# Block-sorted attention and a ResMLP layer on one core: first batch from flat slabs on 64-row array tiles, later batches in a hand-set order

## The chip, the cores and the metric

One NeuronCore of a Trainium2 chip (trn2) runs one program. The metric is device time in microseconds (us); most runs were timed several times and the median is given. The profiled execution has a *span*, from its first to its last instruction, which is some 1.8 us shorter than its time. The *chain* is the work that ended last, followed back from the last instruction to what released it at each step. A run over 1.5% above the fastest of the same kernel counts as slow, and ratios leave slow runs out. A ratio here is the mean time of one kernel's fast runs over that of the other's in the same rounds, so it is not quite the ratio of the medians beside it.

Engines: PE is TensorE (matmul), PEld its weight loads, DVE VectorE, ACT ScalarE, POOL GpSimd, SP SyncE; a trailing q means the engine's DMA queue or sequencer. Every line of the compute engines says L65 because one helper records every instruction; lines are told apart by tile names.

## The reference

Four batches, 8 heads, 768 tokens, 64 per head; the layer is 512 wide with a hidden width of 2048.

```python
P = sort_net                              # (4, 8, 8, 8); five rounds of exp and normalising
k_sorted = einsum('bhij,bhjcd->bhicd', P, k_b)      # mix the 8 blocks of 96 tokens
v_sorted = einsum('bhij,bhjcd->bhicd', P, v_b)
attn = softmax(scale * q_b @ k_sorted^T)            # within each block of 96
x = attn @ v_sorted                                 # -> (4, 768, 512)
a1 = alpha1 * x + beta1
u  = x + lam * einsum('ts,bsd->btd', w_tok, a1)     # token mixing, 768 x 768
a2 = alpha2 * u + beta2
out = u + lam * (relu(a2 @ w_ch1) @ w_ch2)          # "h" is the first wide layer, "ch" the second
```

`lam` is folded into the second layer's weights: W2 is scaled once, on the chip, before the first ch.

## The kernel before

All of batch 0's attention, the preparation of w_tok and W2 and batch 1's first loads share the first 80 us. After that, layers of one batch alternate with attention of the next.

```python
load_q(0); load_raw(0, 1); load_raw(0, 0)             # GpSimd issues the first loads; k and v go f32 -> f16 in the DMA
...                                                    # w_tok, lam, alpha, beta
load_raw(1, 1); load_raw(1, 0); load_q(1)              # batch 1's data go ahead of the weights
...
def prep_w2(which):                                    # 16 products, all on GpSimd
    for m in which:
        pool.tensor_tensor(W2p[:, m, :], W2p[:, m, :], lamB[:], ALU.mult)
...
def mix_v(b, alone=False, groups=range(6)):            # V mixed, then to DRAM and back,
    ...                                                # which puts it into rows of 96 tokens
    nc.sync.dma_start(vscr[b, ...], vA[...])
    nc.sync.dma_start(Vs[b % NV][...], vscr[b]...)
...
def moe_turn(b, hf, ps=psb):                           # u turned on TensorE, 12 turns a half
    ...
emit_attention(0, between)                             # TensorE order: batch 0, w_tok turns between
...
prep_w2(range(HT))
moe_h(0, 0)
for b in range(1, B):
    ...
    emit_attention(b); moe_h(b - 1, 0); moe_ch(b - 1, 0); moe_h(b - 1, 1); moe_a(b); moe_ch(b - 1, 1)
```

The softmax here doesn't subtract the row's maximum and nothing guards it: scores larger than these inputs give would overflow.

## Time and profile before

| before | value | how to read it |
|---|---|---|
| time, three runs | 305.71 us (302.97 to 307.75) | device time |
| span of the profiled run | 308.3 us | a slow run by the rule: some 310 us of time, over 2% above 302.97 |
| TensorE busy | 276.1 us, 90% | the rest of the span is waiting |
| first h matmul | 59.2 us | from the chain in the prediction below |
| first ch matmul | 77.4 us | start of its second stretch there |
| one steady batch | 64.2 us | third row of its stretches |

Two rows of the page's DMA list matter as well (what was moved, issuing queue, count, size, us from issue to landing): W2's pieces and the way of V back from DRAM.

```profile
W2p<-in_moe_w_ch_dram POOLq DMA_DIRECT2D x4, 512.0 KB, 19.1
Vs_107<-vscr SPq DMA_DIRECT2D x4, 384.0 KB, 7.2
```

The 19.1 us are mostly queueing behind older loads: at the 207 GB/s that the prediction reads from that stretch, 512 KB would take some 2.5 us (an estimate). The median of V's way back is 7.2 us, while the prediction found one of 20.14 us.

### The profile page before, as it was taken

What the parts mean: (1) busy time and instruction counts of PE and PEld (TensorE: products, weight loads), DVE (VectorE), ACT (ScalarE), POOL (GpSimd) and SP (SyncE); (2) the same over time, 40 slices, a digit from 0 to 9 for tenths busy, and PEclk for the clock granted to TensorE, in tenths of its full rate; (3) what the DMA queues carried; (4) which work ended last, traced back from release to release, by engine and by line L of the source; (5) the groups of instructions that cost most, each with busy time, mean ns of one, the idle gap of its engine ahead of it and who ended that gap; (6) DMA issues with size and microseconds to landing.
All of it is one profiled execution on the core that took longest, in us unless ns stands there. A gap on an engine that the chain in (4) does not pass through costs nothing.

```text
span 308.3 us, 5117 instructions
## 1 busy us (share of the span) xinstructions
PE 276.1 (90%) x1965; PEld 164.0 (53%) x1965; DVE 180.5 (59%) x414; ACT 153.3 (50%) x327; POOL 104.2 (34%) x106
## 2 busy tenths in 40 slices
PE   3858997699959998999999989989999889999994
PEld 2547774365527554456755544566646444554641
DVE  7779578699936939669684089295840571001001
ACT  4894854384314555349713745197407450631710
POOL 8514569999540460240019300510085000000000
PEclk9968979699997999999999999999999999999999
DMA  5999999929993210592302002950021002102012
GB/s 198 211 237 257 204 208 205 201 59 125 157 226 126 86 52 0 138 152 21 102 20 86 0 2 65 147 97 0 2 70 37 0 0 70 34 0 79 26 34 68
DMA packets 33208, 29.31 MB, mean 95 GB/s; under 512 B 20184, under 2 KB 28192, under 8 KB 33184
## 3 DMA queue, kind: packets, MB, share of 16 engines
q0 software_dynamic: 8112, 14.82, 24.9%
q1 hardware_dynamic: 25072, 14.17, 23.0%
q8 instruction: 15, 0.25, 0.3%
q14 instruction: 9, 0.07, 0.1%
HBM read 32.78 MB, written 8.65 MB: 134 GB/s over the span
## 4 chain that ended last, share of the span: by engine, by line
PE 63%; DMA 19%; DVE 7%; ACT 5%; POOL 2%; issue 2%; SPq 0%; DVEq 0%; POOLq 0%; ACTq 0%
PE ch_ps L65 25%; PE h_ps L65 24%; DMA Vs_107<-vscr 7%; DMA b1lB<-in_moe_beta_dram 6%; PE tok_ps L65 5%; DMA qn_127<-in_q_dram 3%; PE x_ps L65 3%; ACT kT L65 3%; PE sc_ps L65 3%; DVE toktmp L65 2%; DMA raw_88<-in_v_dram 2%; DVE u_0_723 L65 2%; PE uT_ps L65 2%; DMA vscr<-vA 2%; PE v_ps L65 1%
## 5 line engine op out<-in xcount | busy, mean ns | idle before, releaser
L65 ACT ACTIVATE hTa<-h_ps 128x384 bf16<-128x384 f32 x96 | 46.7, 496 | 60.6 <-PE h_ps L65 59.8
L65 PE MATMUL ch_ps<-W2p,hTa 128*128 128x512 bf16 x288 | 72.4, 382 | 0.0
L65 PEld LDWEIGHTS <-W1p 128*128 128x128 bf16 x512 | 49.6, 99 | 32.0 <-issue 2.8
L65 PEld LDWEIGHTS <-hTa 128*128 128x128 bf16 x288 | 27.5, 99 | 27.3
L65 ACT ACTIVATE et<-sc_ps 96x384 f16<-96x384 f32 x64 | 27.0, 497 | 19.7 <-PE sc_ps L65 19.5
L65 DVE TENSOR_TENSOR toktmp<-tok_ps,a1lB 128x512 f32<-128x512 f32 x24 | 16.5, 686 | 30.6 <-PE tok_ps L65 30.6
L65 DVE CAST kT<-k_ps 64x256 f16<-64x256 f32 x72 | 30.3, 421 | 2.2 <-PE k_ps L65 1.1
L65 ACT CAST kT<-k_ps 64x256 f16<-64x256 f32 x48 | 17.6, 366 | 17.9 <-PE k_ps L65 17.2
L65 PEld LDWEIGHTS <-w_tokT 128*128 128x128 f16 x198 | 17.4, 101 | 15.7 <-issue 1.5
L65 PE MATMUL ch_ps<-W2p,hTb 128*128 128x512 bf16 x96 | 25.1, 379 | 0.0
L65 PEld LDWEIGHTS <-kT 128*96 128x96 f16 x160 | 17.0, 141 | 9.0 <-issue 2.3
L65 POOL TENSOR_TENSOR W2p<-W2p,lamB 128x512 bf16<-128x512 bf16 x16 | 20.5, 1316 | 0.1
L65 PEld LDWEIGHTS <-et 96*96 96x96 f16 x256 | 15.9, 129 | 8.4 <-issue 4.5
L65 DVE RECIPROCAL recip<-x_ps 96x4 f32<-96x4 f32 x64 | 9.9, 169 | 17.2 <-PE x_ps L65 16.9
L65 ACT ACTIVATE hTb<-h_ps 128x384 bf16<-128x384 f32 x32 | 15.7, 491 | 5.9 <-PE h_ps L65 5.3
L65 PEld LDWEIGHTS <-hTb 128*128 128x128 bf16 x96 | 9.3, 98 | 10.5
L65 PE MATMUL h_ps<-a2T_730,W1p 128*128 128x384 bf16 x64 | 14.4, 362 | 0.3 <-ACT a2T_730 L65 0.2
L65 PE MATMUL h_ps<-a2T_2377,W1p 128*128 128x384 bf16 x64 | 12.4, 326 | 0.0
L65 PE MATMUL h_ps<-a2T_1573,W1p 128*128 128x384 bf16 x64 | 12.4, 326 | 0.0
L65 PE MATMUL x_ps<-Vs_107,et 96*96 96x65 f16 x128 | 8.5, 213 | 3.5 <-DMA Vs_107<-vscr 3.4
L65 PE MATMUL h_ps<-a2T_731,W1p 128*128 128x384 bf16 x64 | 10.7, 326 | 0.0
L65 PE MATMUL h_ps<-a2T_1574,W1p 128*128 128x384 bf16 x64 | 10.6, 326 | 0.0
(272 smaller groups left out, 448.6 us busy)
## 6 DMA issues: line engine op xcount, KB each, us to landing
out_dram<-ost SPq DMA_DIRECT2D x24, 192.0 KB, 2.2
qf<-in_q_dram SPq DMA_DIRECT2D x8, 384.0 KB, 5.1
vscr<-vA SPq DMA_DIRECT2D x6, 384.0 KB, 4.4
W1p<-in_moe_w_ch_dram POOLq DMA_DIRECT2D x4, 512.0 KB, 14.6
W2p<-in_moe_w_ch_dram POOLq DMA_DIRECT2D x4, 512.0 KB, 19.1
Vs_107<-vscr SPq DMA_DIRECT2D x4, 384.0 KB, 7.2
out_dram<-ost SPq DMA_DIRECT2D x24, 64.0 KB, 2.0
wt_109<-in_moe_w_tok_dram POOLq DMA_DIRECT2D x1, 864.0 KB, 15.7
```

Of the source, the lines that this page charges most:

```text
L65: ins = getattr(self.eng, name)(*args, **kwargs)
```

## The change

The intent is an earlier start of the wide layers and fewer TensorE cycles per batch. Batch 0 is loaded as flat slabs and turned, mixed and scored on 64-row tiles of the array, two at once, with *filler* matmuls on zeros (`warm`) wherever TensorE would wait. Batch 1's loads move behind the weights. W2's scaling is split between GpSimd and VectorE. Later batches still mix k and turn q on TensorE; u is now turned in the DMA, the scores run on 64-row tiles, and every small piece is hung by hand behind a chosen piece of a wide layer (`put`). The diff, cut:

```diff
-    load_q(0)
-    load_raw(0, 1)
-    load_raw(0, 0)
+    load_slabs(q8, q)
+    load_slabs(k8, k)
+    load_halves(v8, v[0])
+    for half in range(2):          # w_tok in two halves; the second lives in the buffer of "qn"
+        t_ = att.tile([128, 3, S], F16, name="wt16", tag=("mixed", "qn")[half], bufs=1)
...
+    def warm(n):
+        ps = pse([128, 512], FT, "warm_ps")
+        for _ in range(n):
+            pe.matmul(ps[:], wz[:, 0:128], wz[:], start=True, stop=True)
+
+    def turn_slab(src, rhs, g, name, ps):            # 24 matmuls of 64x64, alternating tiles
+        for s in range(12):
+            for h2 in range(2):
+                t = (s + 6 * h2) % 12
+                r = slice(h2 * 64, h2 * 64 + 64)
+                pe.matmul(ps[r, t // 6, ...], src[r, g, t * D:(t + 1) * D], rhs(r, g), ...)
+
+    def v_sort(n, eng):                              # v: token-major to column-major, a quarter
+        eng(
+            VD[:, n * 16:(n + 1) * 16, 0:HB].rearrange("p d t -> p t d"),
+            v8[:, :, n * 16:(n + 1) * 16],
+        )
...
-    def moe_turn(b, hf, ps=psb):                     # 12 turns on TensorE
+    def moe_cross(b, hf):
+        for m in range(3):
+            nc.sync.dma_start_transpose(uT[:, :, m * 128:(m + 1) * 128], u16_of[b][:, 3 * hf + m, :])
...
+    score(0, 0, 0, psd)
+    k_copy(0, 2, kp2, 1, copy)
+    v_sort(1, act.copy)                              # the four v_sorts alternate with exponentials on ScalarE
+    score(0, 0, 1, psd)
...
+    load_kv(1)
+    load_q(1)                                        # needs the "qn" buffer
...
+    put(0, 0, "h", 6, ... second_u(kt))              # GpSimd: row, then addition, three times
+    put(0, 0, "h", 7, *(lambda n=n: mix_matrix(n) for n in range(1, B)))
+    for n in range(4):
+        put(0, 0, "h", 11 + n, lambda n=n: scale_w2((4 * n, 4 * n + 1), pool),
+                               lambda n=n: scale_w2((4 * n + 2, 4 * n + 3), dve))
+    for b in range(1, B):
+        p = b - 1
+        put(p, 0, "h", 15, lambda b=b: bounce_v(b))  # V to DRAM
+        put(p, 0, "c", 2, lambda b=b: back_v(b))     # and back
+        if b + 1 < B:
+            put(p, 0, "c", 2, lambda b=b: load_kv(b + 1), lambda b=b: load_q(b + 1))
...
```

## The prediction

> **What bounds the kernel now.** I read the page's slices first, then the engines by stretch, then the chain of the start, then GpSimd's timeline.
>
> ```profile
> PE   3858997699959998999999989989999889999994
> PEclk9968979699997999999999999999999999999999
> DMA  5999999929993210592302002950021002102012
> ```
>
> Forty slices of 7.7 us. From the ninth slice (62 us) on TensorE is nearly full but for the twelfth; earlier it has holes and a lowered clock, and the DMA row is full from slice 2 to 8. So there are two regimes, a start bound by something else and a long TensorE-bound rest.
>
> ```profile
> core 0: us, PE busy (x) PEld busy (x) DVE busy (x) ACT busy (x) POOL busy (x), PEclk, DMA share, GB/s
> 30.00:60.00 30.00, 24.05 (x242) 16.85 (x241) 20.96 (x49) 17.95 (x37) 24.08 (x25) 0.87 1.21 208
> 77.40:101.60 24.20, 20.73 (x171) 12.87 (x170) 16.64 (x41) 7.33 (x18) 7.51 (x8) 0.93 0.86 161
> 165.90:230.10 64.20, 62.05 (x438) 35.99 (x436) 38.36 (x87) 33.31 (x73) 16.84 (x13) 1.00 0.29 51
> ```
>
> The last row is one whole batch in the steady state: TensorE idles 2.1 of 64.2 us. There only fewer TensorE cycles can help.
>
> ```profile
> 11.67 18.12 DMA b1lB<-in_moe_beta_dram
> 30.07 10.10 DMA qn_127<-in_q_dram
> 40.45 0.74 POOL W2p L65
> 41.21 1.28 POOL a1lB L65
> 42.49 1.23 POOL b1lB L65
> ...
> 48.44 4.94 DVE u_0_723 L65
> ...
> 59.21 3.04 PE h_ps L65 x9
> ```
>
> The chain of the start (start, us, what). The first wide layer (h) begins only near 59 us, and it is held by GpSimd: its multiplications of two small vectors stand behind weight-DMA issues, which in turn wait for older loads.
>
> ```profile
> 38.59 0.74 POOL L65 DMA_DIRECT2D W2p<-in_moe_w_ch_dram  x1 [1.27 <-DMA qn_127<-in_q_dram]
> 40.45 0.74 POOL L65 DMA_DIRECT2D W2p<-in_moe_w_ch_dram  x1 [1.12 <-DMA qn_127<-in_q_dram]
> 52.92 20.52 POOL L65 TENSOR_TENSOR W2p<-W2p,lamB 128x512 bf16<-128x512 bf16 x16
> ```
>
> GpSimd's timeline. Counting its DMAs in issue order, number n waits for the landing of number n-8 (the W2 issue that is the 28th waits for the 20th, a q half). Then it scales W2 in 16 steps of 1.28 us, until 73.4 us. The second layer (ch), which needs W2, starts at 77.4 us.
>
> **What the Trainium skill says.** "TensorEngine Tiling (Array Packing)", Key Properties: different tiles load weights and multiply in parallel, but changing the tiling mode drains the engine. No 64-row tile runs before, so the trace cannot agree or not. "TensorE: Matmul & The Clock Gate", Part 1: the clock is halved when idle and released by some 3.4 us of activity; the low digits of PEclk in the start agree in kind. "SBUF — State Buffer", Who interferes with whom: a DVE operation with two SBUF inputs contends with GpSimd's reads. The trace agrees: the same 512-wide f32 addition took 4.94 us at 48.4 us, beside GpSimd, and 0.69 us in later batches. "DMA: Bandwidth & Descriptors", Constraints: the transpose in DMA takes 2-byte data and is issued from Sync or Scalar only; no transfer before shows its time.
>
> **The change, part by part.**
>
> *Steady part, TensorE.* A layer half is 64 h matmuls in 10.40 us and 48 ch matmuls in 10.36 us (the chain at 273 to 304 us), so a batch is 4 x 10.4 = 41.5 us; token mixing is 36 x 0.216 = 7.8 us. Neither changes. Before, a batch also has 6 value-mixing matmuls of 512 columns (1.3 us), 24 key-mixing and 24 q-turning ones of 128 columns (about 0.056 us each, 1.35 us each set), 32 scores of 192 columns at 0.08 (2.6), 64 attention-times-V at 0.044 (16 took 0.71 in the chain: 2.8) and 24 turns of u (1.35): 10.7 us. Sum 60.1; the measured 64.2 leaves 4.1 of waits. After, the turns of u go to the DMA for all but the first half of batch 0 (-1.35 us a batch), and the scores become 64 matmuls of half the width on 64-row tiles; at the 0.044 us of the similar V matmuls that is 2.8, the same. So 9.6 us. I add 1.5 us a batch for draining at some 16 changes of tiling mode (an estimate of 0.1 us each: half of the 0.2 us that one short turn takes alone here, as nothing before shows a drain) and 2 us for waits, since h (16 x 0.496 = 7.9 us of ScalarE) now shares its stretch with 8 exponentials of 768 elements (about 0.77 us, by the slope from 384 elements at 0.497 to 512 at 0.588): 14.1 us of ScalarE against 16 us of TensorE is close. A batch becomes about 62.5 us instead of 64.2. The hand-set order mostly fills the same time; it is not a large gain in the steady state, apart from the first V bounce (20.14 us of DMA at 72 to 92 us in the chain), which before left some 3.5 us of hole in TensorE.
>
> *Start, TensorE.* The chain of 5 normalisations of the sort matrix (done at 11.5 us) stays. Flat slabs of batch 0 are turned in 64-row tiles, two at once; v is mixed straight into the V layout (no kT turn, no 4 x 0.69 us copy). I count about 96 q, 96 k, 128 v, 64 score and 96 V small matmuls at 0.035 to 0.044 us (18 us), 54 turns of w_tok at 0.077 (4.2), token mixing with its additions (6), fillers (39 x 0.216 plus a cold first dozen, 10) and 1.5 of the rest: about 40 us from 1.2 us on. So h can start at 40 to 44 us instead of 59. DVE's own sum to there is about 27 us and ScalarE's about 30, so neither is worse. The fillers occupy only time in which TensorE waits; they may cost a little where a release comes early and buy the full clock.
>
> *Start, transfers.* In f32-to-16-bit loads the DMA row runs at about 207 GB/s of destination. q, k, v, w_tok, W1 and W2 are 3 x 0.79 + 1.18 + 2.1 + 2.1 MB, two broadcasts 0.5: 8.3 MB, 40 us, so W2 has landed by about 43 us instead of 60, because batch 1's loads now come after it. Then the halves of batch 1's v land at about 45 and 47, of k at 49 and 51, q at 54.
>
> *Start, GpSimd: where I think the gain is cut.* Batch 1's four k, v and six q issues stand in GpSimd's order ahead of its elementwise work. By the n-8 rule the last q issues wait for the first kv transfers, 47 us. Only then come, for the second half of batch 0, three rows of 1.56 and three additions of 1.16 (8.2 us, to 56) and GpSimd's half of the W2 scaling, 8 x 1.28 = 10.3 us, to about 66.5. The other 8 are DVE's. With h at 42 us, h plus what is hung into it (18 w_tok turns 1.4, column sums 1.04, token mixing 3.9, value mixing 1.3 us) ends at 61; the first ch piece (3.45 us) then waits at its 14th matmul for the scaled W2 until about 67 and ends at 67.6. Before, ch began at 77.4, so its first piece ended at about 81. The start therefore gains 13 us, not the 17 of h.
>
> *Sum.* From 67.6: layers 166 - 10.4 - 3.45 = 152.3; token mixing of three batches 23.6; attention 9.6 x 3 - 1.3 = 27.5; drains 4.5; waits 6. That is 213.9 (before: 223 from the same point). TensorE ends at 281.5; the last addition and store took 4.2 us before. Span about 285.7 against 308.3, ratio 0.927. On the median of 305.71 this is 283; I shade it to 282 because the waits are the softest term.
>
> **Rivals.**
> - *GpSimd does not hold the start.* If its elementwise work comes in time, ch begins when h ends: first piece done at about 64 instead of 67.6, and a faster TensorE start (h at 35 us, tiles truly two at once) then counts fully: 270 to 275. For it: the order was set by hand. Against it: the kernel before has just such a hold on its chain, 18.12 and 10.10 us.
> - *Fillers and mode drains eat the gain.* If each filler delays real work and the small matmuls run at the 0.08 us of those before instead of 0.04, the start needs 55 us and h begins as late as before; with three batches of scores at 0.08 too (+7 us): 295 to 302. Against it: 16 V matmuls took 0.71 us.
> - *The DMA transposes come late.* After the third token piece TensorE has two ch pieces, 6.9 us, until the next h. Multiply 0.69, add 0.70, copy 0.63 and four affine steps of 0.25 leave about 3.9 us for a transfer; out stores took 2.2. If three 128 KB transposes queue for 8 us, each of three batches loses about 4 us: 294.
> - *Scaled W2 or V arrives even later* (batch 1's V bounce meeting batch 2's loads, as in the 20.14 us before): +3 to +8 us.
>
> **Range and chances.** The ideal (no holds, no drains) is near 268; the rivals that add up lie at 294. So 282, with 270 to 293 for eight in ten. To stay within 2% the time would have to exceed 299.6, which needs two of the bad rivals together: 4%; slower by 2%: 1%; faster: 95%.
>
> **What would show it.** The first h matmul at 40 to 44 us; GpSimd idle on batch-1 transfers just ahead of its rows for the second half; its W2 scaling ending at 65 to 68 us and the first ch group waiting on it; ch's first piece done near 68. Steady batches of 62 to 63 us with full clock, no turn of u on TensorE after batch 0, score matmuls at 0.04 us spacing. PEclk near 9 in all early slices. Wrong would be: h later than 48 us, transposes over 4 us with TensorE idle before h, or a steady batch over 64 us.

## The result, and the profile after

| | time, median | fast runs against before | span | TensorE busy |
|---|---|---|---|---|
| before, with the later runs | 306.73 us (302.97 to 313.11) | | 308.3 | 276.1 |
| after, 4 runs | 326.99 us (325.00 to 329.54) | 1.0744, 95% interval 1.0666 to 1.0822 | 323.2 | 279.4 |

The change made the kernel 7% slower. The prediction was 282 us with a range to 293: wrong in its sign.

The slices of the kernel after, 40 of 8.1 us each:

```profile
PE   6964897987089628999999899999998999999994
PEclk9985699799679776999999999999999999999998
DMA  6999992091009991013228990321590013202112
```

From the seventeenth slice on (129 us), TensorE is full. Earlier there are three troughs: slices 3 and 4, with a clock that falls to 5, slices 10 and 11 with an idle DMA, and slices 14 and 15 with a full DMA. The stretches around them (length, then busy us and instructions of PE, PEld, DVE, ACT, POOL, then clock, DMA share, GB/s), with one steady batch last:

```profile
20.00:40.00 20.00, 12.39 (x218) 8.82 (x220) 5.39 (x6) 16.57 (x13) 10.05 (x13) 0.57 1.21 211
...
57.00:90.00 33.00, 20.96 (x145) 11.46 (x146) 23.06 (x37) 9.12 (x20) 26.30 (x22) 0.83 0.43 37
...
102.00:123.00 21.00, 10.43 (x86) 5.78 (x86) 2.14 (x3) 9.35 (x16) 15.60 (x14) 0.77 1.45 177
...
150.30:211.90 61.60, 60.08 (x441) 33.57 (x443) 31.05 (x56) 32.69 (x59) 24.40 (x22) 1.00 0.67 103
```

TensorE idles 7.6, 12.0 and 10.6 us in the first three rows and 1.5 us in the steady batch. A steady batch takes 61.6 us against 64.2 before, with a granted clock of 1.00 in both rows, so the part that was to gain does gain; the loss lies ahead of it. In each trough another engine is busy: ScalarE in the first (16.57 of 20 us), VectorE and GpSimd in the second, the DMA in the third.

**First hold: four copies.** The chain that ended last, from 16.83 us on (start, us, what):

```profile
16.83 3.64 ACT vd L65
20.47 0.64 ACT et L65
21.11 3.53 ACT vd L65
24.64 0.64 ACT et L65
25.28 3.50 ACT vd L65
28.78 0.64 ACT et L65
29.42 3.50 ACT vd L65
32.91 0.65 ACT et L65
```

For 16.7 us the chain never leaves ScalarE. `vd` is the quarter copy of v (`v_sort`), `et` an exponential of the scores. TensorE's v mixing needs `vd`, and its next pieces need a buffer in PSUM, the memory that TensorE writes to, that an exponential has to empty; the trace names `vd` for 5.3 us of weight loads' waiting and `et` for 4.9 us of the v mixing's. The group row gives 3613 ns for one copy:

```profile
L65 ACT COPY vd<-v 128x768 f16<-128x768 f16 x4 | 14.5, 3613 | 0.0
```

The first h matmul comes at 57.25 us instead of the predicted 40 to 44. In the chain:

```profile
57.25 0.81 PE h_ps L65 x4
...
91.56 3.56 PE ch_ps L65 x13
```

The second line ends the first ch piece.

**Second hold: GpSimd's order, and W2 scaled by two engines at once.** GpSimd's timeline (start, us, instruction, and in brackets the idle time before it and what ended it), and below it VectorE's over the same stretch:

```profile
37.80 1.05 POOL L65 DMA_DIRECT2D raw<-in_k_dram  x2
62.76 5.31 POOL L65 DMA_DIRECT2D qn<-in_q_dram  x6 [23.91 <-PE wtok_ps L65]
...
76.07 1.17 POOL L65 TENSOR_TENSOR u<-x,u 128x512 f32<-128x512 f16 x1
77.20 12.11 POOL L65 TENSOR_TENSOR W2p<-W2p,lamB 128x512 bf16<-128x512 bf16 x8
```

```profile
78.83 9.47 DVE L65 TENSOR_TENSOR W2p<-W2p,lamB 128x512 bf16<-128x512 bf16 x6
88.22 1.21 DVE L65 CAST mixed<-mix_ps 128x1024 f16<-128x1024 f32 x1
89.35 1.28 DVE L65 TENSOR_TENSOR W2p<-W2p,lamB 128x512 bf16<-128x512 bf16 x2
```

GpSimd stands for 23.9 us in front of batch 1's q loads, because their destination is the buffer that holds w_tok's second half, and TensorE turns that half only behind the first h pieces (the last turn ends at 62.46). Then follow 5.3 us of issues, three rows and additions, and only at 77.2 us the scaling of W2. It runs beside VectorE's half, at 1545 and 1401 ns per piece. VectorE's copy of the mixed V stands behind its six and TensorE waits for it until 89.5 us; the first ch piece ends at 95.1 us instead of the predicted 67.6.

**Third hold: V's way back.** In the chain it is one piece:

```profile
102.08 20.05 DMA Vs<-vscr
```

The DMA issues between 90 and 130 us (size, median us to landing) show what it shared the engines with:

```profile
raw<-in_v_dram POOLq DMA_DIRECT2D x2, 384.0 KB, 9.2
Vs<-vscr SPq DMA_DIRECT2D x1, 768.0 KB, 20.1
raw<-in_k_dram POOLq DMA_DIRECT2D x2, 384.0 KB, 8.2
qn<-in_q_dram POOLq DMA_DIRECT2D x6, 128.0 KB, 12.1
```

Batch 2's loads, 2.3 MB at their destination, were issued at 96.7 to 110.7 us. TensorE has nothing to multiply the attention with until 122.2.

What held as predicted, or went better: 24 matmuls of 64x64 took 0.49 us on the chain, 0.02 us each where 0.035 to 0.044 was assumed; eight scores with their change of mode take 0.28 to 0.50 us on the chains, mostly 0.31, so 0.04 each; and the DMA transposes land in 2.3 us (at most 4.2), with VectorE waiting for them 13.8 us in all and TensorE never named as waiting for them.

```profile
uT<-u SPq DMA_TRANSPOSE x21, 2.3
```

### The profile page after: what moved, and what is told of

The parts are those of the page before. It is cut to its first block, busy times and chain, and to the rows that moved or that the text cites. A ratio compares the mean times of both kernels' runs of the same rounds, so it can differ in the third digit from the quotient of the medians.

```text
span 323.2 us, 5632 instructions
## 1 busy us (share of the span) xinstructions
PE 279.4 (86%) x2308; PEld 157.5 (49%) x2322; DVE 152.7 (47%) x296; ACT 148.6 (46%) x255; POOL 120.9 (37%) x121
## 4 chain that ended last, share of the span: by engine, by line
PE 71%; ACT 11%; DMA 8%; DVE 5%; POOL 3%; issue 2%; SPq 0%; DVEq 0%; POOLq 0%
PE ch_ps L65 25%; PE h_ps L65 22%; PE tok_ps L65 9%; DMA Vs<-vscr 6%; ACT vd L65 4%; PE x_ps L65 4%; DVE W2p L65 3%; POOL u L65 3%; ACT et L65 2%; PE wtok_ps L65 2%; PE sc_ps L65 2%; DMA q<-in_q_dram 2%; ACT kT L65 1%; PE warm_ps L65 1%; ACT hTa L65 1%
## 5 line engine op out<-in xcount | busy, mean ns | idle before, releaser
L65 PE MATMUL h_ps<-a2T,W1p 128*128 128x384 bf16 x512 | 99.0, 335 | 6.8 <-DVE ost L65 3.2
L65 POOL TENSOR_TENSOR u<-x,u 128x512 f32<-128x512 f16 x24 | 30.8, 1310 | 41.8 <-DVE x L65 38.3
L65 PEld LDWEIGHTS <-hTa 128*128 128x128 bf16 x288 | 28.1, 99 | 32.9 <-issue 2.2
L65 POOL TENSOR_SCALAR u<-b1lB,rs 128x512 f32<-128x512 f32 x21 | 33.0, 1606 | 28.9 <-DVE ost L65 28.9
L65 DVE TENSOR_TENSOR ost<-ch_ps,u 128x512 f32<-128x512 f32 x24 | 16.6, 690 | 48.0 <-PE ch_ps L65 42.9
L65 PE MATMUL tok_ps<-x,w_tokT 128*128 128x512 f16 (+1 forms) x198 | 34.3, 321 | 1.6 <-DVE toktmp L65 1.0
L65 ACT ACTIVATE et<-sc_ps 96x768 f16<-96x768 f32 (+1 forms) x32 | 27.3, 853 | 13.1 <-PE sc_ps L65 12.9
L65 ACT CAST kT<-kmix_ps 64x512 f16<-64x512 f32 x27 | 19.1, 708 | 29.6 <-PE kmix_ps L65 15.2
L65 POOL DMA_DIRECT2D qn<-in_q_dram x18 | 15.9, 913 | 23.9 <-PE wtok_ps L65 23.9
L65 PE MATMUL x_ps<-Vs,et 96*96 96x65 f16 (+2 forms) x288 | 17.8, 210 | 7.4 <-DMA Vs<-vscr 7.4
L65 PEld LDWEIGHTS <-et 96*96 96x96 f16 (+2 forms) x288 | 16.6, 124 | 12.1 <-DMA Vs<-vscr 7.8
L65 DVE TENSOR_TENSOR u<-toktmp,u 128x512 f32<-128x512 f32 x21 | 18.8, 897 | 2.8 <-POOL u L65 0.7
L65 PE MATMUL sc_ps<-qT,kT 64*96 64x96 f16 (+1 forms) x256 | 13.4, 225 | 6.1 <-ACT et L65 4.1
## 6 DMA issues: line engine op xcount, KB each, us to landing
W2p<-in_moe_w_ch_dram POOLq DMA_DIRECT2D x4, 512.0 KB, 16.8
```

The costliest lines, as they stand in the source:

```text
L65: ins = getattr(self.eng, name)(*args, **kwargs)
```

## The experiments

The theory after the result: three holds, (a) the strided v copies on ScalarE, (b) GpSimd's order ahead of W2's scaling, which also lets both halves run at once, (c) the loads beside V's way back, and nothing in the new steady state. The rivals: the fillers or the new array modes cost the time; or the holds hide one another, so that mending one moves the wait to another place. Eleven kernels ran, all correct. In each group "before" was timed on the same chip; its medians there were 310.6, 308.4, 305.4 and 303.9 us, with slow runs among them. The kernel after was not timed again in these groups; a gain in us below is a difference of medians between groups and good to some 1 to 2 us.

### One copy in each form (m1_sorts)

```diff
-        eng(VD[..., quarter n].rearrange("p d t -> p t d"), v8[:, :, quarter n])
+        if n in (0, 2): eng(VD[..., quarter n], v8[:, :, quarter n].rearrange("p t d -> p d t"))
+        else:           eng(VD[..., quarter n].rearrange("p d t -> p t d"), v8[:, :, quarter n])
-    v_sort(2, act.copy)     # and v_sort(3, act.copy)
+    v_sort(2, copy)         # and v_sort(3, copy): VectorE
```

The elements are the same; only the order in which they are visited changes: with contiguous writes the 2-byte reads step by 128 bytes, in the original the writes do.

> A measurement of the disputed cost: the four copies that re-sort the v slab (128x768, 16-bit, SBUF to SBUF) took 3.61 us each on ScalarE in the changed kernel, where I had counted under 0.8. Here the first runs on ScalarE with contiguous writes and strided reads, the second on ScalarE as before (strided writes), the third on VectorE with contiguous writes, the fourth on VectorE with strided writes. Theory 'stride of the write': the first about 0.9 us, the second 3.6, the third 0.9 or less, the fourth over 2 us. Rival 'any stride is slow': all four 3 us or more. Rival 'ScalarE alone is slow': first and second 3.6, third and fourth 0.9. The first h matmul moves from 57 us to 48-52 us if two copies become cheap, and stays at 57 if TensorE itself set the start.

ScalarE's timeline of this run, contiguous writes first, then strided:

```profile
16.97 1.52 ACT L65 COPY vd<-v 128x768 f16<-128x768 f16 x1
...
19.11 3.68 ACT L65 COPY vd<-v 128x768 f16<-128x768 f16 x1
```

And VectorE's, again contiguous first:

```profile
21.48 0.87 DVE L65 COPY vd<-v 128x768 f16<-128x768 f16 x1
...
25.47 1.87 DVE L65 COPY vd<-v 128x768 f16<-128x768 f16 x1
```

On ScalarE strided writes cost 2.4 times as much as strided reads; the contiguous form was expected at 0.9 us and took 1.52. On VectorE one copy each says nothing firm, because contiguous ones took 0.80 to 1.87 us in later runs, and the strided one took 1.87, under the expected 2. The one look took 316.12 us, h began at 48.5 us.

### All four copies on VectorE, contiguous (a_sort)

```diff
-            VD[...].rearrange("p d t -> p t d"), v8[:, :, ...],
+            VD[...], v8[:, :, ...].rearrange("p t d -> p d t"),
-    v_sort(0, act.copy)     # and 1, 2, 3
+    v_sort(0, copy)         # and 1, 2, 3
```

> Only the four v copies change: VectorE instead of ScalarE, with contiguous writes (0.87 us there in the measurement, against 3.61). Theory 'ScalarE's copies set the start': h begins at 45 to 49 us instead of 57, and since GpSimd's q issues follow TensorE's w_tok turns after h, the whole chain moves with it: ch begins at 79-83 us instead of 90.3, time 315-319. Rival 'TensorE itself sets the start' (as my prediction's 40 us of TensorE work and the mode drains would have it): h at 53 us or later, time 322 or more.

313.07 us (312.14 to 314.08), ratio 1.037 (1.026 to 1.048): 13.9 us less than the change. h begins at 47.6 us, and the clock is full through the first 60 us. So (a) is real: it accounts for 9.6 of the 15.2 us by which h was late. The first ch comes 11.3 us earlier (79.0 against 90.3), since the second hold starts earlier too: GpSimd begins to scale W2 at 65.9 us instead of 77.2. This kernel changes the engine and the order of the writes together; the run before it tells the two apart for one copy, not for the time.

### Batch 2's loads later (c_loads)

```diff
-            put(p, 0, "c", 2, lambda b=b: load_kv(b + 1), lambda b=b: load_q(b + 1))
+            put(p, 1, "h", 7, lambda b=b: load_kv(b + 1), lambda b=b: load_q(b + 1))
```

> Only the place of the next batch's k, v and q loads changes: they are issued in the middle of the second h stretch of the batch, after V has come back from DRAM, not beside it. Theory 'contention': V's way back takes under 10 us from issue to landing instead of 20.1, the TensorE holes of 7.4 us before the first V matmul of batch 1 and of 3.2 us behind the stalled output stores vanish, and the time falls by 8 to 12 us to 315-319. Rival 'the 128-byte pieces are slow by themselves': V still takes about 20 us and the time stays within 2 us of 327.

V's way back, in the DMA issues of this run between 95 and 130 us:

```profile
Vs<-vscr SPq DMA_DIRECT2D x1, 768.0 KB, 7.8
```

314.84 us (311.97 to 316.32), ratio 1.036 (1.021 to 1.051): 12.2 us less than the change, although in the profiled run h even came late (61.5 us; nothing before h was edited, so h varies by some 4 us between executions of this start). The Trainium skill's page "DMA: Bandwidth & Descriptors", Queues, rings and completion order, says that each DMA engine goes round its queue rows at packet granularity. The runs agree in kind: the same transfer took 7.8 us with only output stores issued near it and 20.05 us beside GpSimd's queue.

### GpSimd's scaling before the q issues (b_w2early)

```diff
     load_kv(1)
+    for m in (0, 1, 4, 5, 8, 9, 12, 13):
+        pool.tensor_tensor(W2p[:, m, :], W2p[:, m, :], lamB[:], ALU.mult)
     load_q(1)
-    ... scale_w2((4 * n, 4 * n + 1), pool), scale_w2((4 * n + 2, 4 * n + 3), dve)
+    ... scale_w2((4 * n + 2, 4 * n + 3), dve)
```

> Only GpSimd's order changes: its 8 scalings of W2 come right after batch 1's k and v issues, in the 24 us in which it stood idle before the q issues, not after the rows of the second half. Theory 'GpSimd holds ch': ch begins at 79-82 us instead of 90.3 and the time falls by 7 to 11 us to 316-320. Rival 'the chain over the rows and u copies holds it': ch begins at 87 us or later and the time falls by under 3 us. Rival 'contention': VectorE's two-input operations of the start get slower and h begins at 59 us or later, eating part of it.

GpSimd's timeline of this run:

```profile
38.79 6.77 POOL L65 TENSOR_TENSOR W2p<-W2p,lamB 128x512 bf16<-128x512 bf16 x6
45.80 2.29 POOL L65 TENSOR_TENSOR W2p<-W2p,lamB 128x512 bf16<-128x512 bf16 x2 [0.24 <-DMA W2p<-in_moe_w_ch_dram]
62.19 5.35 POOL L65 DMA_DIRECT2D qn<-in_q_dram  x6 [14.10 <-PE wtok_ps L65]
```

W2 is landing then, its last piece for GpSimd at 45.8 us, so the eight products fit into time in which GpSimd had stood idle, at about 1.15 us each. 318.54 us (fast runs 317.2 to 319.2), ratio 1.048 (1.037 to 1.059): 8.5 us less. The first ch comes at 83.1 us, a little later than expected: the rows and VectorE's half still end late. VectorE's half in this run:

```profile
L65 DVE TENSOR_TENSOR W2p<-W2p,lamB 128x512 bf16<-128x512 bf16 x8 | 5.0, 684 | 0.0
```

What changed in the chain is VectorE's half: its first six pieces start at 77.4 us instead of 78.8 and take 3.7 us instead of 9.5. That is 7.2 us, as much as ch comes earlier (83.1 against 90.3). So GpSimd's half held ch mostly by slowing VectorE's half beside it; in the kernel after, the trace names no wait of TensorE for GpSimd's own pieces. The rows in GpSimd's order still set when VectorE can start.

### Without fillers (d_nofill, abcd_nofill, abcde_nofill)

```diff
     def warm(n):
+        return
```

> All 39 filler matmuls are left out, nothing else. Theory 'fillers are neutral': they lie in waits, and the start is set by ScalarE's copies, so h still begins at 56-59 us and the time stays within 3 us of 327; the granted clock of 0-20 us falls from 1.0 to 0.6-0.8, and small matmuls there take longer without being waited for. Rival 'fillers delay real work': h begins 3 us or more earlier and the time falls by 3 us or more. Rival 'fillers are needed': h begins 3 us or more later.

327.11 us (324.4 to 327.8), ratio 1.0745 (1.060 to 1.089): no change against 326.99. In its profiled run h began at 60.5 us, which meets the mark of the rival "fillers are needed" (3 us or more later); but c_loads, with the same start and its fillers, had h at 61.5, so one start does not decide this. The expected fall of the clock in the first 20 us did not come; the profile gives a clock of 1.00 for this stretch with fillers and without. Yet the matmuls themselves were slower, as TensorE's timelines of the kernel after and then of this run show for the first turns of q:

```profile
6.60 0.56 PE L65 MATMUL q_ps<-ident,q 64*64 64x64 f16 x24 [1.27 <-DMA q<-in_q_dram]
```

```profile
6.51 1.49 PE L65 MATMUL q_ps<-ident,q 64*64 64x64 f16 x48 [6.51 <-DMA q<-in_q_dram]
```

Twice 0.56 is 1.12, against 1.49 for the same 48 without warming. The fillers do buy speed, some tenths of a microsecond in each set of turns, but then the sort matrix and the loads are what TensorE waits for. The same edit on two mended kernels that follow below:

> The former without any filler matmul. With ScalarE's copies gone TensorE's clock in the start counts. Theory 'fillers now pay': h begins 2 to 5 us later, the granted clock of 0-40 us falls, the time rises by 2 to 5 us. Rival 'fillers are neutral', as in the changed kernel (327.1 against 327.0): within 1.5 us.

> The same without fillers, again because two of four runs without them fell in the slow state. Theory 'fillers are neutral even now': fast runs within 1.5 us of those with fillers. Rival 'they buy the clock': 2 to 4 us slower, h 3 us or more later. Rival 'they delay work': 1.5 us or more faster.

The first is inconclusive: 294.87 us with two slow runs of four; its fast runs were 291.72 and 292.59. The second, with five rounds, gave 289.87 us (fast runs 288.88 to 290.25), ratio 0.949 (0.946 to 0.953), where the same kernel with fillers gave 0.946 (0.942 to 0.949). The medians differ by 1.1 us and the two intervals overlap, and h came at 46.6 us against 46.0: the fillers are worth about 1 us or nothing, and they are not the loss.

### The three edits together (abc)

> The three mends together: v copies on VectorE with contiguous writes, GpSimd's W2 scalings in its idle time before the q issues, batch loads after V's return. Theory 'three separate holds': the gains add, 8-10 us (copies) + 7-9 (W2) + 11-14 (V), so 296 to 301 us, 2 to 4% faster than the kernel before; h at 46-49 us, ch at 70-74. Rival 'they overlap': with one hold removed the next one takes its place, 305 us or more.

The edit is a_sort, b_w2early and c_loads in one kernel. 294.43 us (292.51 to 297.15, the longest of them slow), ratio 0.972 (0.960 to 0.984). The three gains of 13.9, 8.5 and 12.2 sum to 34.6; together they are 32.6. In the ratios, each taken within its own group, the steps down from 1.074 are 3.7, 2.7 and 3.8 points, together 10.2, and the kernel with the three edits stands 10.2 lower. They hardly hide one another: the holds lie one behind the other in time. This sets aside the rival of one hold behind another.

### GpSimd's rows and VectorE's scaling moved (abcd)

```diff
     def second_u(kt):
-        moe_row(0, kt)                                                  # GpSimd
+        act.activation(u_of[0][kt], b1lB[:], AF.Copy, scale=rs[:, kt:kt + 1])
...
-        put(0, 0, "h", 11 + n, lambda n=n: scale_w2((4 * n + 2, 4 * n + 3), dve))
+        put(0, 0, "h", 3 + n, lambda n=n: scale_w2((4 * n + 2, 4 * n + 3), dve))
```

> As the three mends together, and two more: the rows of the second half are made by ScalarE (0.72 us each in the kernel before) instead of GpSimd (1.6), and VectorE's 8 scalings of W2 come in its idle time at the fourth to seventh h unit instead of at the twelfth to fifteenth. Theory 'the rest between h and ch is GpSimd's and VectorE's queue': ch begins 19-22 us after h (the 18.7 us that I counted of TensorE's own work) instead of 24 or more, time 3 to 6 us below the three mends, 290 to 297. Rival: TensorE's own work fills it, less than 1.5 us gained.

291.36 us (290.94 to 292.74), ratio 0.965 (0.958 to 0.972). From h to ch it is now 22.8 us (47.5 to 70.3) against 25.8 in abc; 19 to 22 was expected. The ratio's interval overlaps that of abc, so the 3.1 us between the medians are likely, not certain.

### Copies shared out, later mixing matrices later (abcde)

```diff
-    v_sort(0, copy)          # and 2
+    v_sort(0, act.copy)      # and 2; contiguous writes
-    put(0, 0, "h", 7, *(lambda n=n: mix_matrix(n) for n in range(1, B)))
+    put(0, 0, "h", 7, lambda: mix_matrix(1))
+    for n in range(2, B):
+        put(0, 1, "h", 3 * n, lambda n=n: mix_matrix(n))
```

> The five mends and two small ones: of the four v copies two go back to ScalarE, but with contiguous writes (1.52 us there), because VectorE had become the chain between 17 and 27 us; and the mixing matrices of the last two batches are made in the next h stretch, because VectorE's queue held TensorE some 3 us at 56 to 65 us. If VectorE's queue is what is left of the start: h at 45-46 us instead of 47.5, ch 20 us after h or less, time 286-289. If TensorE's own work with the fillers is what is left: h at 47 us or later, time 290-292.

288.76 us (287.40 to 289.35, five rounds), ratio 0.946 (0.942 to 0.949): a mended version now beats both kernels. From h to ch it is 21.8 us, where 20 or less was expected. W2's two halves no longer run side by side:

```profile
L65 POOL TENSOR_TENSOR W2p<-W2p,lamB 128x512 bf16<-128x512 bf16 x8 | 9.1, 1188 | 0.0
L65 DVE TENSOR_TENSOR W2p<-W2p,lamB 128x512 bf16<-128x512 bf16 x8 | 4.9, 683 | 0.0
```

Per piece, 1188 and 683 ns against 1545 and 1401 in the change. Side by side the 16 products took from 77.2 to about 90.6 us, 13.4 us, a copy of 1.2 us among VectorE's; one set behind the other they are 9.1 + 4.9 = 14.0 us. Running the two halves at once gained next to nothing. At 683 ns VectorE alone would need 10.9 us for all 16 (an estimate; no run tried it).

### Batch 1's mixing matrices earlier (abcdef)

In abcde one 128x64 product on VectorE took 3.84 us. Its timeline, then GpSimd's:

```profile
56.45 0.22 DVE L65 TENSOR_REDUCE red<-sel 128x8 f32<-128x64 f32 x1
56.71 3.84 DVE L65 TENSOR_TENSOR bigV<-mhi,red 128x64 f16<-128x64 f16 x1
```

```profile
56.98 3.47 POOL L65 TENSOR_TENSOR u<-x,u 128x512 f32<-128x512 f16 x3
```

It ended when GpSimd's three additions had ended. The first ch piece in the chain of abcde:

```profile
68.00 3.45 PE ch_ps L65 x16
```

The edit moves the product to where GpSimd only issues transfers:

```diff
-    put(0, 0, "h", 7, lambda: mix_matrix(1))
+    put(0, 0, "h", 2, lambda: mix_matrix(1))
```

> Batch 1's mixing matrices move five pieces of the first wide layer earlier, to a point where GpSimd only issues transfers; nothing else differs from the best kernel so far (288.8 us). There, one VectorE instruction of that block, 128x64, took 3.84 us while GpSimd did three additions; others of its form took about 0.25. Theory A: it was held by GpSimd's reads. Then it takes under 0.5 us here, the first ch piece starts near 65 instead of 68.0 us, and the time falls by 2 to 3 us, to about 286. Rival B: GpSimd's additions themselves hold the second half's token pieces, so that VectorE would only have waited elsewhere: the first ch piece stays at 67 to 68.5 us and the time at 288 to 289.

VectorE's timeline of this run, then its chain:

```profile
50.13 0.23 DVE L65 TENSOR_TENSOR bigV<-mhi,red 128x64 f16<-128x64 f16 x1
```

```profile
64.10 3.45 PE ch_ps L65 x16
```

286.43 us (285.04 to 287.21, five rounds), ratio 0.945 (0.940 to 0.950). The first ch starts at 64.1 us instead of 68.0. The ratio hardly differs from abcde's (0.946), because the fast runs of before were themselves shorter in this group (a mean near 303 against 305); the direct sign is the step in the chain, 3.9 us. Theory A holds for the 3.84 us. That the whole gain of 2.3 us in the medians is due to it is not shown, as the two kernels did not run in the same rounds. It is the fastest kernel by its median. Its slices:

```profile
PE   6999997999989999999999999999899999999994
PEclk9999999999999999999999999999999999999999
```

The troughs of the kernel after are gone, and the clock is full throughout.

## Why the prediction was wrong

The profiled span was predicted at 285.7 us and was 323.2, a gap of 37.5 us. It splits at the prediction's own marks: h came 15.2 us late (57.2 against 42); from h to the end of the first ch piece it took 37.9 us instead of 25.6, 12.3 more; the rest took 224 us instead of 213.9, 10 more.

1. **The step that failed first: "DVE's own sum to there is about 27 us and ScalarE's about 30, so neither is worse."** As a sum it was not far off, by luck: ScalarE was busy 32.9 us and VectorE 29.6 us in the first 57 us of the kernel after. The term that failed inside it is the four v copies, which the prediction does not list. The expectation of m1_sorts says that one was counted at under 0.8 us, so some 3.2 for four; they took 14.5, and the rest of ScalarE's work was less than counted. The second fault is that the sum was held against the whole 40 us, while 26.1 of the 32.9 us came after 16.8 us, where they stand in ScalarE's order behind the copy of the mixed k. Between 16.8 and 33.6 us ScalarE worked without a gap, 14.2 us of it on the copies, and TensorE was busy for 8.4. Contiguous writes on VectorE brought h back by 9.6 of the 15.2 us and the time by 13.9. TensorE's own sum was right: up to h it was busy 39.7 us in abcdef, where 40 was predicted, but with waits h comes at 45.7 there. The Trainium skill's page "SBUF — State Buffer", Door 1: The DMA port swizzle, says that SBUF has lines of 16 bytes and that crossing to a new line for each access costs, so that bf16 data may be stepped by eight elements for free. The copies step their writes by 64, and the prediction did not look this up. The runs agree for ScalarE's writes (3.68 against 1.52 us); reads that step just as far cost less there, and no run shows that the crossing of lines is the mechanism.

2. **The GpSimd hold was foreseen, its start was not.** "By the n-8 rule the last q issues wait for the first kv transfers, 47 us." What they waited for was a buffer: w_tok's second half, released by TensorE at 62.5 us. In three kernels the q issues begin 0.3 us after the last w_tok turn has ended (62.46 and 62.76, 51.09 and 51.38, 49.32 and 49.62; in the last, abcdef, the trace names a small matmul just behind the turn). Since those turns stand behind the first h pieces, the late h of step 1 also pushed this hold back. The scaling was sized at 1.28 us per piece; beside VectorE's half it took 1545 ns, and VectorE's 1401 instead of 683. The prediction had cited the contention of the two engines and then not applied it to the very products that the change lays side by side, and b_w2early shows that this slowing was most of what GpSimd's half cost (5.8 of the 7.2 us by which ch came earlier). It had W2 scaled at 66.5 us; that came about 24 us later.

3. **"Scaled W2 or V arrives even later ... +3 to +8 us" was a listed rival, and it came, larger.** V's way back took 20.05 us, the figure that the prediction had read in the kernel before. Moving the loads away was worth 12.2 us. The sum of 213.9 us had left it out; without the contention the rest is 211 to 212 us (211.9 from 71.45 to 283.35 in abcde, and 211.9 from 67.55 to 279.48 in abcdef).

What was right: a steady batch of 62.5 us (61.6); scores at 0.04 us; transposes that TensorE does not wait for; fillers that do not cost much (that they buy the full clock is not shown: the clock of the first 20 us was 1.00 without them). "W2 has landed by about 43 us" was close: GpSimd, given the order for it, scaled from 38.8 us on and waited for the last piece until 45.8. The rival of fillers and drains did not come: 24 turns took 0.49 us.

One reading of the kernel before was off: its first ch piece did not end at about 81 us but shares its stretch with q turns and scores, and VectorE adds its output at 85.5. The gain of 13 us in the start was read against that mark; the sum to 285.7 does not use it.

The sums for the mended kernel come out close, in part by luck. The first ch piece ends at 67.55 us in abcdef, where the prediction had 67.6, but h comes there 3.7 us later than its 42 and the way from h to that end is 3.7 us shorter, because the wait for W2 that it counted is gone. The span is 283.7 against 285.7. The gain that the prediction saw in the change exists; the kernel as given did not reach it. What stays open is why the granted clock fell to 0.57 while TensorE starved at 20 to 40 us, and how much of the 13.9 us is the clock and how much the waiting: no run parted them.

## What to carry to other kernels

Hold an engine's work against the stretch in which its inputs exist, not against the whole span, and look for a copy that writes 2-byte elements far apart. Before moving an issue in an in-order engine's program, ask which buffer it fills and who empties it; everything behind it waits for that. Work with two inputs that is split between VectorE and GpSimd may take as long as one half behind the other (13.4 against 14.0 us here), and a store to DRAM that is read back wants a time of its own, away from bulk loads.

## What the Trainium skill lacked or had wrong

- "SBUF — State Buffer", Door 1: gives the rule of 16-byte lines but no cost for ScalarE or VectorE, nor by side. On ScalarE a 128x768 copy of 2-byte data took 3.61 us with writes 128 bytes apart and 1.52 us with reads 128 bytes apart: the writing side is the dear one.
- "SBUF — State Buffer", Who interferes with whom: right, and a size is missing. Two streams of two-input products slowed each other to 1545 ns (1188 apart) and 1401 ns (683 apart). A 128x64 product of 0.23 us was held for 3.84 us, across three GpSimd additions.
- "TensorE: Matmul & The Clock Gate", Part 1: agrees that early matmuls are slower without activity before them (48 turns in 1.49 us against 24 in 0.56). The granted clock in the profile does not show this: it read 1.00 in both kernels, so the durations have to be read, not that row. The page itself warns that such clock records were found unreliable on trn2.
- "DMA: Bandwidth & Descriptors", Queues, rings and completion order: agrees in kind; it gives no figure for what sharing between two queue rows costs. Here 768 KB took 7.8 us without and 20.05 us beside 2.3 MB of GpSimd's loads.
- "TensorEngine Tiling (Array Packing)", Key Properties: parallel tiles fit the runs (64x64 matmuls at 0.02 us each, where those of 128 columns took 0.056). No figure for the drain is given; eight scores with their change of mode mostly took 0.31 us, and the drain is at most a part of that. No run separates it.
